# Attention, experts and feed-forward on one core: last four attention blocks as one group, first operands prepared in pieces from step 17 on

## The chip, the cores and the metric

The kernel runs on one core of one Trainium2 chip. The metric is the device time of one execution in microseconds (us); the time given for a kernel is the median of its runs. Five engines of the core matter: PE (TensorE, the matmuls), DVE (VectorE), ACT (ScalarE), POOL (GpSimd) and SP (SyncE, which issues the DMAs). Each engine works through its own list of instructions in order and waits on semaphores for the others.

## The reference

Three stages follow each other. Attention has 2 batches, 8 heads, 576 positions of 64 values, and a bias that a small network computes from the positions; its output is 1152 tokens of 512 values. Then come 8 experts whose weights P are normalised in both directions, and last a feed-forward layer with an ELU.

```python
scores = scale * np.matmul(q, k.transpose(0, 1, 3, 2))
x = (psi_rel / psi_i)[..., None]
bias = np.maximum(x @ w1 + b1, 0.0) @ w2
attn = softmax(scores + bias)
x = np.matmul(attn, v)

for e in range(E):
    h = np.maximum(x @ w1[e], 0.0)
    out += P[:, e:e + 1] * (h @ w2[e])

h = x @ w_in
return np.where(h > 0.0, h, np.exp(np.minimum(h, 0.0)) - 1.0) @ w_out
```

## The kernel before, in words

**Attention in 40 steps.** Two heads form a pair; a pair of one batch is a block, and there are 8 blocks. A block has five query tiles, t = 0 to 3 with 128 rows and t = 4 with 64. One step works on one tile of one block. `groups` lists the blocks that are interleaved: first the four blocks of pairs 0 and 1 (steps 0 to 19, tiles in the order 4, 0, 1, 2, 3), then the two blocks of pair 2 (steps 20 to 29) and the two of pair 3 (steps 30 to 39), tiles 0 to 4.

**What a step does.** `run_step(s)` reads a string letter by letter, and each letter puts instructions on the engines' lists; the order is thus written out by hand. For the scores of step s: `R` and `S` (`emit_ttr`) add the bias on DVE and find the maximum, `E` and `F` (`emit_exp`) take the exponentials of the two heads on ACT, which also sum them. For step s - 1: `T` (`emit_tr`) transposes the exponentials on PE; ACT copies one half of them out of PSUM, and `U` copies the other on DVE. `V` (`emit_trl`) transposes the last 64 columns into one of the two buffers that `T` needs next; ACT empties it at once, behind `F`. For step s - 2 there are five pieces of the product with v, one for each `a`; the fifth also multiplies by the reciprocals of the sums (PE `av<-csb,rc`, line 1332). `X` (`x_evac`) then takes the product out: ACT copies the reciprocals (`xf`), DVE multiplies into the token tile `xt`. `Q` (`emit_qk`) is the score product of step s + 1. `N` (`emit_norm`) makes the reciprocals: GpSimd adds a small number to the sums, and DVE takes the reciprocal at once (line 1265), both for step s - 1; they are used a step later.

**Steps 0 to 13 also compute the bias** for all positions: `H` the hidden layer (`ht`, on DVE or ACT as `pick` decides), `M` its product on PE (`bps`), `O` the copy out of PSUM (`o`, on DVE or ACT) and to DRAM. The string is ORD_S in steps 0 to 2, ORD_A until the bias is complete (steps 3 to 13), and ORD_B from step 14 on. In ORD_A the order on DVE is X, R, S, U, O, H, N, V, H; on PE it is T, a, a, M, a, a, a, V, M, Q.

**First operands of the experts.** Every product runs in three parts of high and low halves. `w_split` prepares one tile of the first expert's weights (`w1h`, `w1l`), `ops_first` one of the token operands (`oh`, `ol`): four sums on GpSimd, four copies to the high half on ACT, four subtractions on DVE for the low half. These are queued in `bg`, and `do_bg` sends one piece for each letter `p`, of which ORD_B has two. The two weight tiles are queued after steps 27 and 28, the two token tiles after steps 35 and 37. What is still queued at the end is sent in one go by `first_fill`, which then starts the planner's list of the experts. `prep` converts q and k of a block (two casts on DVE, two subtractions on DVE or, for blocks 4 to 7, on GpSimd).

```python
ORD_A = "XROTSUapaMEaOHaNpaFLVMHQ"
ORD_B = "RTSNUXaafLEafaappFVQ"
elif x == "N" and 1 <= s <= NS:
    emit_norm(s - 1)
```

Of the kernel before, what the change touches and what calls it, by code (L numbers as in the profile page):

```python
# [34 lines left out]
BD = 1  # L35
PRO = "HHPOH0PpOHpPOHPOkkBHHppPkkppOQmHO"
LQ = [100, 101]
LS = [5, 9, 13, 21]
LV = [0, 1, 2, 3, 19, 20, 28, 32]
ACC = [2.6, 3.1]  # L40
WARM = 8
PS = [[1, 0], [2, 1], [3, 2], [4, 13], [5, 16], [6, 20], [7, 26]]
ORD_S = "RMXTSOHUapaMEOHaaNpMFOHaLVQ"
ORD_A = "XROTSUapaMEaOHaNpaFLVMHQ"
ORD_B = "RTSNUXaafLEafaappFVQ"
TOFF = [0, 128, 256, 384, 512]
TROW = [128, 128, 128, 128, 64]
NN = [256, 320]
# [174 lines left out]
def attention_moe_elu_ffn_kernel(  # L223
# [85 lines left out]
    def w_split():  # L309
        (kind, he, j), t = raw_q.pop(0)  # L310
        hi, lo = wt0[he, j] = w1_new()
        st = stp.tile([128, 4, 2, 128], F32, tag="st", name="st")

        def sums():
            for i in range(4):
                w1_sum(t, st, i, pool)

        def part(i):
            if i:
                dst, src = w1_src(t, st)[i - 1]  # L320
                dve.tensor_tensor(out=lo[:, dst], in0=src, in1=hi.bitcast(F32)[:, dst], op=ALU.subtract)
            if i < 4:
                dst, src = w1_src(t, st)[i]
                act.activation(out=hi[:, dst], in_=src, func=ACTF.Copy)

        bg.extend([sums] + [lambda i=i: part(i) for i in range(5)] + [raw_load])

    def ops_new(n):
        p = xp if n == 0 else pools["ops1"]
# [19 lines left out]
    def ops_first(t):  # L349
        if not ops0:  # L350
            ops0.extend(ops_new(0))
        oh, ol = ops0
        i0, i1 = XPAIR[t]
        xa, xb = ops_view(0, t, xt[i0], xt[i1])
        c = slice(128 * t, 128 * t + 128)
        st = stp.tile([128, 4, 2, 128], F32, tag="st", name="st")

        def part(i):
            if i:
                o, src = ops_src(xa, xb, st)[i - 1]  # L360
                dve.tensor_tensor(out=ol[:, o, :, c], in0=src, in1=oh.bitcast(F32)[:, o, :, c], op=ALU.subtract)
            if i < 4:
                o, src = ops_src(xa, xb, st)[i]
                act.activation(out=oh[:, o, :, c], in_=src, func=ACTF.Copy)

        def sums(i):
            ops_sum(xa, xb, st, i, pool)
            ops_sum(xa, xb, st, i + 1, pool)

        bg.extend([lambda: sums(0), lambda: sums(2)] + [lambda i=i: part(i) for i in range(5)])  # L370

    plan = Plan(0.1)
    eng = {"A": act, "D": dve, "P": pool, "S": sp}
# [750 lines left out]
    emit_it = emit()  # L1124


    groups = [[(hp, b) for hp in (0, 1) for b in range(B)]] + [[(hp, b) for b in range(B)] for hp in range(2, HP)]
    blocks = [hb for grp in groups for hb in grp]
    steps = [(hp, b, t) for i, grp in enumerate(groups) for t in (TO if i == 0 else range(5)) for hp, b in grp]
    gorder = [g for t in TO for g in range(8 * t, min(8 * t + 8, GRP))]  # L1130
# [4 lines left out]
    def attention(fill):  # L1135
# [124 lines left out]
        def emit_norm(s):  # L1260
            sm = etile[s][2]
            r = TROW[steps[s][2]]
            rc = tp.tile([128, 2], F32, tag="rc", name="rc")
            pool.tensor_scalar(rc[0:r], sm[0:r], EPS, None, ALU.add)
            dve.reciprocal(rc[0:r], rc[0:r])
            rcs[s] = rc

        def emit_tr(s):
            r = TROW[steps[s][2]]
# [37 lines left out]
        def av_pieces(s):  # L1307
            hp, b, t = steps[s]
            r = TROW[t]
            box = {}  # L1310

            def piece(j):
                def f():
                    if j == 0:
                        box["p"] = av_p[0] = psC[s % 2 if no[0] == GRP else 0]("av")
                    p = box["p"]
                    vt = vts[hp, b]
                    a = aT[s]
                    for h in range(2):
                        pe.matmul(  # L1320
                            p[64 * h:64 * h + 64, 0:r],
                            vt[:, j - 1 if j else 4, 64 * h:64 * h + 64],
                            a[:, 4 * h + j - 1 if j else 8, 0:r],
                            start=(j == 0),
                            stop=(j == 4),
                            skip_group_check=True,
                        )
                    if j == 4:
                        n, o = XN[b][t], 64 * b if t == 4 else 0
                        rc = rcs.pop(s)  # L1330
                        for h in range(2):
                            pe.matmul(  # L1332
                                p[64 * h:64 * h + 64, 128:128 + r],
                                rc[0:r, h:h + 1].to_broadcast([r, 64]),
                                ident[0:r, 0:r],
                                start=True,
                                stop=True,
                                skip_group_check=True,
                            )
                        ev_q.append((p, r, hp, n, o))  # L1340
                        aT.pop(s)
                return f

            return [piece(j) for j in range(5)]
# [18 lines left out]
        def run_step(s):  # L1363
            d = s - LAG
            cur, tr = s < NS, 0 <= d < NS
            for x in ORD_S if s < 3 else ORD_A if no[0] < GRP else ORD_B:
                if x == "T" and tr:
                    emit_tr(d)
                elif x == "U":
# [6 lines left out]
                elif x in "RS" and cur:  # L1376
                    emit_ttr(s, "RS".index(x))
                elif x in "EF" and cur:
                    emit_exp(s, "EF".index(x))
                elif x == "N" and 1 <= s <= NS:  # L1380
                    emit_norm(s - 1)
                elif x == "X":
                    x_evac()
                elif x == "a":
                    av(1)
                elif x == "M":
                    bias_p()
                elif x == "O":
                    bias_o()
                elif x == "H":  # L1390
                    bias_hh()
                elif x == "p":
                    for _ in range(3 if s < 4 else 1):
                        prep_next()
                    do_bg(1)
                elif x == "L":
                    bias_loads(s)
                elif x == "f":
                    fill_pe(s)
# [139 lines left out]
        for s in range(NS + LAG):  # L1539
# [9 lines left out]
            for i, s0 in PS:  # L1549
                if s == s0:  # L1550
                    prep_q.append(prep(i))
            run_step(s)
            if no[0] < GRP:
                load["a"] += ACC[0]
                load["d"] += ACC[1]
            if s >= NS:
                left.close()
                filler = fill()
                continue
            if s in (20, 22, 24):  # L1560
                raw_load()
            if s == 27:
                w_split()
            if s == 28:
                w_split()
            if s == 15:
                w = csb[:, C_WG:C_WG + 4 * E].rearrange("p (k e) -> p k e", k=4)
                dve.tensor_copy(wg_hl[:, :, 0:E], w)
                dve.tensor_tensor(out=wg_hl[:, :, E:2 * E], in0=w, in1=wg_hl.bitcast(F32)[:, :, 0:E], op=ALU.subtract)
            if s == NS - 5:  # L1570
                ops_first(0)
            if s == NS - 3:
                ops_first(1)
        while av_q:
            x_evac()
            av(3)
# [77 lines left out]
```

## Time and profile before

| | |
|---|---|
| median of 3 runs | 1155.81 us (1154.01 to 1160.21) |
| the profiled execution | 1160.57 us |
| its span | 1158.8 us |
| PE busy | 1127.2 us (97%) |
| DVE busy | 894.3 us (77%) |
| ACT busy | 617.5 us (53%) |
| POOL busy | 48.2 us (4%) |
| mean granted TensorE clock | 0.989 |

The profiled execution takes 1160.57 us, of which its span, from the first to the last instruction, is 1158.8. Attention lies in the first 195 us of it; the rest is the experts and the feed-forward layer. A busy share is an average over the whole span: PE at 97% may still wait in one stage, and an engine that is seldom busy may be the one that others wait for.

### The profile page before, as it was taken

What the parts mean: (1) busy time and instruction counts of PE and PEld (TensorE: products, weight loads), DVE (VectorE), ACT (ScalarE), POOL (GpSimd) and SP (SyncE); (2) the same over time, 40 slices, a digit from 0 to 9 for tenths busy, and PEclk for the clock granted to TensorE, in tenths of its full rate; (3) what the DMA queues carried; (4) which work ended last, traced back from release to release, by engine and by line L of the source; (5) the groups of instructions that cost most, each with busy time, mean ns of one, the idle gap of its engine ahead of it and who ended that gap; (6) DMA issues with size and microseconds to landing.
All of it is one profiled execution on the core that took longest, in us unless ns stands there. A gap on an engine that the chain in (4) does not pass through costs nothing.

```text
span 1158.8 us, 20865 instructions
## 1 busy us (share of the span) xinstructions
PE 1127.2 (97%) x8080; PEld 984.8 (85%) x8080; DVE 894.3 (77%) x1929; ACT 617.5 (53%) x1417; POOL 48.2 (4%) x85
## 2 busy tenths in 40 slices
PE   7899999999999999999999999999999998999998
PEld 3467878988889999999998989998989887989896
DVE  7797887846788888887887878877665568888865
ACT  7897777743234344444443434443434357876653
POOL 0002132000000000000000000000000001000000
PEclk9899998999999999999999999999999999999999
DMA  6564640210122323223323132232111100111002
GB/s 208 194 222 150 201 132 12 75 58 33 55 65 91 110 92 109 91 92 117 102 92 94 64 125 92 91 110 89 58 38 55 51 24 19 55 37 55 19 1 81
DMA packets 36034, 100.14 MB, mean 86 GB/s; under 512 B 3808, under 2 KB 3936, under 8 KB 35936
## 3 DMA queue, kind: packets, MB, share of 16 engines
q1 hardware_dynamic: 35936, 98.82, 26.4%
q8 instruction: 63, 1.03, 0.4%
q14 instruction: 35, 0.29, 0.1%
HBM read 77.16 MB, written 21.64 MB: 85 GB/s over the span
## 4 chain that ended last, share of the span: by engine, by line
PE 88%; ACT 4%; DVE 3%; issue 1%; DVEq 0%; ACTq 0%
PE y L735 41%; PE m L542 38%; PE av L1320 3%; PE sc L1229 2%; PE tr L1281 2%; ACT et L1256 1%; PE bps L1452 1%; ACT ht L1434 1%; PE av L1332 1%; PE trl L1300 0%; ACT o L1484 0%; PE lg L890 0%; ACT aT L1287 0%; DVE ol L442 0%; PE x2t L984 0%
## 5 line engine op out<-in xcount | busy, mean ns | idle before, releaser
L542 PE MATMUL m<-oh,w1h 128*128 128x256 f32 (+1 forms) x1120 | 331.1, 296 | 1.2 <-ACT u L555 1.2
L542 PE MATMUL m<-ol,w1h 128*128 128x256 f32 (+1 forms) x1120 | 330.3, 295 | 0.1
L542 PE MATMUL m<-oh,w1l 128*128 128x256 f32 (+1 forms) x1120 | 329.9, 295 | 0.0
L735 PE MATMUL y<-w2h,hh 128*128 128x512 f32 x720 | 282.2, 392 | 2.3 <-ACT hh L649 1.1
L735 PE MATMUL y<-w2l,hh 128*128 128x512 f32 x720 | 281.6, 391 | 0.8 <-DVE w2l L442 0.8
L735 PE MATMUL y<-w2h,hl 128*128 128x512 f32 x720 | 281.5, 391 | 0.0
L542 PEld LDWEIGHTS m<-oh,w1h 128*128 128x128 f32 x1120 | 211.2, 189 | 9.0 <-ACT u L555 1.7
L542 PEld LDWEIGHTS m<-ol,w1h 128*128 128x128 f32 x1120 | 211.0, 188 | 8.1 <-DVE ol L442 0.6
L542 PEld LDWEIGHTS m<-oh,w1l 128*128 128x128 f32 x1120 | 211.3, 189 | 0.1
L735 PEld LDWEIGHTS y<-w2h,hh 128*128 128x128 f32 x720 | 135.1, 188 | 27.5 <-ACT hh L649 2.0
L735 PEld LDWEIGHTS y<-w2h,hl 128*128 128x128 f32 x720 | 135.2, 188 | 26.7 <-DVE hl L652 0.2
L735 PEld LDWEIGHTS y<-w2l,hh 128*128 128x128 f32 x720 | 135.2, 188 | 24.5 <-DVE w2l L442 1.1
L605 ACT ACTIVATE hh<-c 128x512 fp32r<-128x512 f32 (+3 forms) x128 | 72.0, 563 | 144.9 <-DVE c L574 144.7
L766 DVE SCALAR_TENSOR_TENSOR acc<-y,P,acc 128x512 f32<-128x512 f32 x126 | 94.6, 751 | 65.8 <-PE y L735 64.4
L555 ACT ACTIVATE u<-m 128x256 f32<-128x256 f32 (+1 forms) x160 | 64.9, 405 | 86.2 <-PE m L542 84.4
L555 ACT ACTIVATE p<-m 128x256 f32<-128x256 f32 (+1 forms) x160 | 65.6, 410 | 71.1 <-PE m L542 66.2
L608 DVE SCALAR_TENSOR_TENSOR hl<-c,hh 128x512 fp32r<-128x512 f32 (+3 forms) x128 | 77.7, 607 | 20.1 <-ACT hh L605 17.4
L435 ACT ACTIVATE w2h<-raw 128x512 fp32r<-128x512 f32 x80 | 48.5, 627 | 51.1 <-PE y L735 50.4
L1241 DVE CUSTOM_DVE_ANT_0 et<-sc,bt 128x576 f32<-128x576 f32 (+1 forms) x80 | 57.2, 752 | 17.1 <-PE sc L1229 15.3
L435 ACT ACTIVATE w1h<-st 128x512 fp32r<-128x512 f32 x76 | 46.5, 623 | 33.9 <-DVE st L307 32.2
L1256 ACT ACTIVATE et<-et,nmx 128x576 f32<-128x576 f32 (+1 forms) x80 | 61.8, 776 | 0.7 <-DVE nmx L1241 0.7
L574 DVE TENSOR_TENSOR c<-m,u 128x256 f32<-128x256 f32 (+1 forms) x80 | 36.6, 457 | 32.2 <-PE m L542 29.6
(140 smaller groups left out, 1516.4 us busy)
## 6 DMA issues: line engine op xcount, KB each, us to landing
raw<-w1p SPq DMA_DIRECT2D x32, 512.0 KB, 3.9
raw<-w2p SPq DMA_DIRECT2D x32, 512.0 KB, 3.3
scr<-o SPq DMA_DIRECT2D x36, 295.5 KB, 2.5
bt<-scr SPq DMA_DIRECT2D x16, 576.0 KB, 4.3
cw<-w1d SPq DMA_DIRECT2D x16, 512.0 KB, 4.1
wsc<-ca SPq DMA_DIRECT2D x32, 256.0 KB, 4.0
cw<-w2d SPq DMA_DIRECT2D x16, 512.0 KB, 4.1
raw<-wsc SPq DMA_DIRECT2D x16, 512.0 KB, 3.6
```

The lines of the kernel that those rows point to most:

```text
L435: act.activation(out=dst(bh.get()), in_=src(), func=ACTF.Copy)
L542: lambda e, w=w, o=o, j=j, k=k: pe.matmul(x["ap"](bank), w.get()[:, ai, j, :], o.get()[:, bi, j, :], start=(k == 0 and i in (1, 2, 5)), st ...
L555: lambda e: act.activation(out=b.get()[:, 0:N], in_=x["ap"](bank), func=ACTF.Copy),
L574: lambda e: eng[e].tensor_tensor(out=blk(b.get()[:, half * N:half * N + N], rev), in0=ap(p), in1=ap(q), op=ALU.add),
L605: op([("A", cA(w))], lambda e: act.activation(out=hh(), in_=ap(), func=ACTF.Relu), r=sk, w=wh, after=gate_)
L608: lambda e: dve.scalar_tensor_tensor(out=bl.get()[:, d], in0=ap(), scalar=0.0, in1=hhf(), op0=ALU.max, op1=ALU.subtract),
L735: lambda e, a=a, w=w, f=f, i=i, y=y, c=c: pe.matmul(y.get(), a.get()[:, c], w.get(), start=(f == 0 and i == 0), stop=(f == 3 and i == 2)),
L766: lambda e: dve.scalar_tensor_tensor(out=a.get(), in0=y.get(), scalar=P[0][:, n, e_:e_ + 1], in1=a.get(), op0=ALU.mult, op1=ALU.add),
L1229: pe.matmul(sc[h][0:r, x, 0:HALF], q[d, qc], k[d, kc], start=i == 0, stop=i == 2, tile_position=(64 * h, 0))
L1241: dve.tensor_tensor_reduce(out=e.rearrange("p (x j) -> p x j", x=2), in0=sc[0:r, :, 0:HALF], in1=biast[hp, t][0:r, h].rearrange("p (x j) - ...
L1256: act.activation(out=e, in_=e, func=ACTF.Exp, scale=-1.0, bias=nmx[0:r, h:h + 1], accum_out=sm[0:r, h:h + 1])
L1320: pe.matmul(p[64 * h:64 * h + 64, 0:r], vt[:, j - 1 if j else 4, 64 * h:64 * h + 64], a[:, 4 * h + j - 1 if j else 8, 0:r], start=(j == 0) ...
```

## The change

The four blocks of pairs 2 and 3 become one group of steps 20 to 39: tiles 0 of four blocks, then tiles 1, and so on, so that the four tiles of 64 rows come last. `BG` queues the weight tiles before steps 17 and 22 and the token tiles before steps 27 and 32. A piece is sent by the new letter `g`, one in a step; ORD_B has one `g`, between `E` and `F`, and its two `p` only prepare q and k. The four subtractions of each tile go to GpSimd, and the sums move into the pieces. Loads of q, k, v and of the first weights are issued earlier. `N` still adds on GpSimd for step s - 1, but the reciprocal on DVE, now `emit_recip`, is that of step s - 2, in all three strings. The last step has a string of its own, ORD_E, and the planner's list is started before it, so that its letters `f` send products of the first expert. The products with v of the last two steps use the same PSUM buffer.

```diff
@@ -35,14 +35,16 @@
 BD = 1
 PRO = "HHPOH0PpOHpPOHPOkkBHHppPkkppOQmHO"
 LQ = [100, 101]
-LS = [5, 9, 13, 21]
-LV = [0, 1, 2, 3, 19, 20, 28, 32]
+LS = [5, 8, 11, 14]
+LV = [0, 1, 2, 3, 19, 20, 21, 22]
+BG = [17, 22, 27, 32]
 ACC = [2.6, 3.1]
 WARM = 8
-PS = [[1, 0], [2, 1], [3, 2], [4, 13], [5, 16], [6, 20], [7, 26]]
+PS = [[1, 0], [2, 1], [3, 2], [4, 13], [5, 16], [6, 17], [7, 18]]
 ORD_S = "RMXTSOHUapaMEOHaaNpMFOHaLVQ"
 ORD_A = "XROTSUapaMEaOHaNpaFLVMHQ"
-ORD_B = "RTSNUXaafLEafaappFVQ"
+ORD_B = "RTSNUXaaLEaaappgFVQ"
+ORD_E = "XffTUNaafaaaV"
 TOFF = [0, 128, 256, 384, 512]
 TROW = [128, 128, 128, 128, 64]
 NN = [256, 320]
@@ -316,14 +318,18 @@
                 w1_sum(t, st, i, pool)
 
         def part(i):
-            if i:
+            if i == 0:
+                sums()
+            else:
                 dst, src = w1_src(t, st)[i - 1]
-                dve.tensor_tensor(out=lo[:, dst], in0=src, in1=hi.bitcast(F32)[:, dst], op=ALU.subtract)
+                pool.tensor_tensor(out=lo[:, dst], in0=src, in1=hi.bitcast(F32)[:, dst], op=ALU.subtract)
             if i < 4:
                 dst, src = w1_src(t, st)[i]
                 act.activation(out=hi[:, dst], in_=src, func=ACTF.Copy)
-
-        bg.extend([sums] + [lambda i=i: part(i) for i in range(5)] + [raw_load])
+            else:
+                raw_load()
+
+        bg.extend([lambda i=i: part(i) for i in range(5)])
 
     def ops_new(n):
         p = xp if n == 0 else pools["ops1"]
@@ -356,18 +362,17 @@
         st = stp.tile([128, 4, 2, 128], F32, tag="st", name="st")
 
         def part(i):
+            if i < 2:
+                ops_sum(xa, xb, st, 2 * i, pool)
+                ops_sum(xa, xb, st, 2 * i + 1, pool)
             if i:
                 o, src = ops_src(xa, xb, st)[i - 1]
-                dve.tensor_tensor(out=ol[:, o, :, c], in0=src, in1=oh.bitcast(F32)[:, o, :, c], op=ALU.subtract)
+                pool.tensor_tensor(out=ol[:, o, :, c], in0=src, in1=oh.bitcast(F32)[:, o, :, c], op=ALU.subtract)
             if i < 4:
                 o, src = ops_src(xa, xb, st)[i]
                 act.activation(out=oh[:, o, :, c], in_=src, func=ACTF.Copy)
 
-        def sums(i):
-            ops_sum(xa, xb, st, i, pool)
-            ops_sum(xa, xb, st, i + 1, pool)
-
-        bg.extend([lambda: sums(0), lambda: sums(2)] + [lambda i=i: part(i) for i in range(5)])
+        bg.extend([lambda i=i: part(i) for i in range(5)])
 
     plan = Plan(0.1)
     eng = {"A": act, "D": dve, "P": pool, "S": sp}
@@ -1124,7 +1129,7 @@
     emit_it = emit()
 
 
-    groups = [[(hp, b) for hp in (0, 1) for b in range(B)]] + [[(hp, b) for b in range(B)] for hp in range(2, HP)]
+    groups = [[(hp, b) for hp in hps for b in range(B)] for hps in ((0, 1), (2, 3))]
     blocks = [hb for grp in groups for hb in grp]
     steps = [(hp, b, t) for i, grp in enumerate(groups) for t in (TO if i == 0 else range(5)) for hp, b in grp]
     gorder = [g for t in TO for g in range(8 * t, min(8 * t + 8, GRP))]
@@ -1260,10 +1265,12 @@
         def emit_norm(s):
             sm = etile[s][2]
             r = TROW[steps[s][2]]
-            rc = tp.tile([128, 2], F32, tag="rc", name="rc")
+            rc = rcs[s] = tp.tile([128, 2], F32, tag="rc", name="rc")
             pool.tensor_scalar(rc[0:r], sm[0:r], EPS, None, ALU.add)
-            dve.reciprocal(rc[0:r], rc[0:r])
-            rcs[s] = rc
+
+        def emit_recip(s):
+            rc = rcs[s][0:TROW[steps[s][2]]]
+            dve.reciprocal(rc, rc)
 
         def emit_tr(s):
             r = TROW[steps[s][2]]
@@ -1312,7 +1319,7 @@
             def piece(j):
                 def f():
                     if j == 0:
-                        box["p"] = av_p[0] = psC[s % 2 if no[0] == GRP else 0]("av")
+                        box["p"] = av_p[0] = psC[1 if s >= NS - 2 else s % 2 if no[0] == GRP else 0]("av")
                     p = box["p"]
                     vt = vts[hp, b]
                     a = aT[s]
@@ -1363,7 +1370,7 @@
         def run_step(s):
             d = s - LAG
             cur, tr = s < NS, 0 <= d < NS
-            for x in ORD_S if s < 3 else ORD_A if no[0] < GRP else ORD_B:
+            for x in ORD_S if s < 3 else ORD_A if no[0] < GRP else ORD_B if cur else ORD_E:
                 if x == "T" and tr:
                     emit_tr(d)
                 elif x == "U":
@@ -1377,8 +1384,11 @@
                     emit_ttr(s, "RS".index(x))
                 elif x in "EF" and cur:
                     emit_exp(s, "EF".index(x))
-                elif x == "N" and 1 <= s <= NS:
-                    emit_norm(s - 1)
+                elif x == "N":
+                    if 1 <= s <= NS:
+                        emit_norm(s - 1)
+                    if 2 <= s:
+                        emit_recip(s - 2)
                 elif x == "X":
                     x_evac()
                 elif x == "a":
@@ -1392,6 +1402,7 @@
                 elif x == "p":
                     for _ in range(3 if s < 4 else 1):
                         prep_next()
+                elif x == "g":
                     do_bg(1)
                 elif x == "L":
                     bias_loads(s)
@@ -1549,28 +1560,25 @@
             for i, s0 in PS:
                 if s == s0:
                     prep_q.append(prep(i))
+            if s == NS:
+                left.close()
+                filler = fill()
             run_step(s)
             if no[0] < GRP:
                 load["a"] += ACC[0]
                 load["d"] += ACC[1]
             if s >= NS:
-                left.close()
-                filler = fill()
                 continue
-            if s in (20, 22, 24):
+            if s in (15, 16, 17):
                 raw_load()
-            if s == 27:
-                w_split()
-            if s == 28:
-                w_split()
+            if s + 1 in BG:
+                i = BG.index(s + 1)
+                w_split() if i < 2 else ops_first(i - 2)
             if s == 15:
                 w = csb[:, C_WG:C_WG + 4 * E].rearrange("p (k e) -> p k e", k=4)
                 dve.tensor_copy(wg_hl[:, :, 0:E], w)
                 dve.tensor_tensor(out=wg_hl[:, :, E:2 * E], in0=w, in1=wg_hl.bitcast(F32)[:, :, 0:E], op=ALU.subtract)
-            if s == NS - 5:
-                ops_first(0)
-            if s == NS - 3:
-                ops_first(1)
+        emit_recip(NS - 1)
         while av_q:
             x_evac()
             av(3)
```

How instructions move, in two places. The first is DVE in step 10, from the copy of the transposed exponentials (`aT<-tr`) to that of the last 64 columns (`aT<-av`). The number behind a name tells tiles apart. Before:

```order
L1371 COPY aT_1217<-tr_1219 128x8x64
L1486 TENSOR_SCALAR o_1252<-bps_1244,csb_87 128x176
L1486 TENSOR_SCALAR o_1252<-bps_1244,csb_87 128x415
L1436 TENSOR_SCALAR ht_152<-U_134,csb_87 128x448
L1436 TENSOR_SCALAR ht_153<-U_134,csb_87 128x448
L1265 RECIPROCAL rc_1262<-rc_1262 128x2
L1303 COPY aT_1217<-av_1239 128x64
```

Now:

```order
L1378 COPY aT_1216<-tr_1218 128x8x64
L1497 TENSOR_SCALAR o_1251<-bps_1243,csb_87 128x176
L1497 TENSOR_SCALAR o_1251<-bps_1243,csb_87 128x415
L1447 TENSOR_SCALAR ht_152<-U_134,csb_87 128x448
L1447 TENSOR_SCALAR ht_153<-U_134,csb_87 128x448
L1273 RECIPROCAL rc_1169<-rc_1169 128x2
L1310 COPY aT_1216<-av_1238 128x64
```

Nothing moved but the tile of the reciprocal: it was rc_1262, it is rc_1169. PE's list in the same step uses rc_1169 before and now; this is its part now:

```order
L1463 MATMUL bps_1243<-ht_153,csb_87 32x416
L1463 MATMUL bps_1243<-ht_154,csb_87 32x416 x3
L1327 MATMUL av_1238<-aT_1124,vt_298 64x128 x6
L1339 MATMUL av_1238<-csb_87,rc_1169 64x128 x2
L1307 MATMUL trl_1271<-csb_87,et_1098 128x64
L1307 MATMUL av_1238<-csb_87,et_1098 128x64
L1463 MATMUL bps_1276<-ht_151,csb_87 32x432 x3
L1463 MATMUL bps_1276<-ht_152,csb_87 32x432
```

PE thus reads a reciprocal that DVE made in the step before; now it reads the one that DVE makes in this step, behind the copies `o` and the hidden layers `ht`.

The second place is ACT where the first weight tile is copied. Before, in steps 28 to 30, whose first exponentials are those of the 64-row tiles:

```order
L1256 ACTIVATE et,sm<-et,nmx 64x576
L324 ACTIVATE w1h<-raw 128x512
L1256 ACTIVATE et,sm<-et,nmx 64x576
L1305 ACTIVATE aT<-trl 128x64
L1287 ACTIVATE aT<-tr 128x4x64
L1350 ACTIVATE xf<-av 128x128
L1256 ACTIVATE et,sm<-et,nmx 64x576
L324 ACTIVATE w1h<-raw 128x256
L324 ACTIVATE w1h<-st 128x512
L1256 ACTIVATE et,sm<-et,nmx 64x576
```

Now, in steps 17 and 18:

```order
L1261 ACTIVATE et,sm<-et,nmx 128x576
L328 ACTIVATE w1h<-raw 128x512
L1261 ACTIVATE et,sm<-et,nmx 128x576
L1312 ACTIVATE aT<-trl 128x64
L1294 ACTIVATE aT<-tr 128x8x64
L1357 ACTIVATE xf<-av 128x128
L1261 ACTIVATE et,sm<-et,nmx 128x576
L328 ACTIVATE w1h<-raw 128x256
L1261 ACTIVATE et,sm<-et,nmx 128x576
```

The copies still stand between the two exponentials, one in a step at most, and eleven steps earlier.

## Rows read from the trace of the kernel before

**Rows 1.** DVE's instructions in order of time, step 10: start us, us, engine, what.

```profile
80.33 0.75 DVE L1241 CUSTOM_DVE_ANT_0 et<-sc,bt 128x576 f32<-128x576 f32 x1
...
83.87 0.16 DVE L1265 RECIPROCAL rc<-rc 128x2 f32<-128x2 f32 x1
```

**Rows 2.** PE's instructions in order of time, where step 10 reads its reciprocals.

```profile
82.69 0.39 PE L1332 MATMUL av<-csb,rc 128*64 128x128 f32 x4
```

**Rows 3.** PE's instructions in order of time, end of step 12.

```profile
93.35 0.39 PE L1332 MATMUL av<-csb,rc 128*64 128x128 f32 x4
...
93.88 1.04 PE L1452 MATMUL bps<-ht,csb 128*32 128x496 f32 x8
94.85 0.40 PE L1229 MATMUL sc<-kh,qh 64*128 64x288 f32 x2
```

**Rows 4.** DVE's instructions in order of time: reciprocals of steps 3 and 13, scores of step 13.

```profile
48.85 0.15 DVE L1265 RECIPROCAL rc<-rc 64x2 f32<-64x2 f32 x1
...
95.94 0.76 DVE L1241 CUSTOM_DVE_ANT_0 et<-sc,bt 128x576 f32<-128x576 f32 x1 [0.52 <-PE sc L1229]
...
98.27 0.16 DVE L1265 RECIPROCAL rc<-rc 128x2 f32<-128x2 f32 x1
```

**Rows 5.** DVE then PE in order of time, where PE waits for DVE's `xt`.

```profile
102.13 0.28 DVE L1351 TENSOR_TENSOR xt<-av,xf 128x128 f32<-128x128 f32 x1
...
102.56 1.85 PE L1320 MATMUL av<-aT,vt 128*64 128x128 f32 x20 [1.97 <-DVE xt L1351]
```

**Rows 6.** PE's longest waits in the stretch 105 to 200 us: total, times, longest.

```profile
PE tr L1281 <- ACT aT L1305: 4.4, 7, 0.9
```

**Rows 7.** ACT's instructions in order of time, steps 33 to 35.

```profile
164.68 0.22 ACT L1305 ACTIVATE aT<-trl 128x64 f32<-128x64 f32 x1
...
167.11 1.15 ACT L324 ACTIVATE w1h<-st 128x512 fp32r<-128x512 f32 x2
168.91 0.22 ACT L1305 ACTIVATE aT<-trl 128x64 f32<-128x64 f32 x1
169.93 0.60 ACT L1287 ACTIVATE aT<-tr 128x512 f32<-128x512 f32 x1 [0.80 <-PE tr L1281]
...
172.10 0.22 ACT L1305 ACTIVATE aT<-trl 128x64 f32<-128x64 f32 x1
```

**Rows 8.** DVE in order of time, step 17: reciprocal in ORD_B.

```profile
114.35 0.16 DVE L1265 RECIPROCAL rc<-rc 128x2 f32<-128x2 f32 x1
```

**Rows 9.** PE in order of time: step 17, then the products of a 64-row tile.

```profile
113.56 1.31 PE L1320 MATMUL av<-aT,vt 128*64 128x128 f32 x20
114.70 0.39 PE L1332 MATMUL av<-csb,rc 128*64 128x128 f32 x4
...
189.81 0.80 PE L1320 MATMUL av<-aT,vt 128*64 128x64 f32 x20
190.54 0.33 PE L1332 MATMUL av<-csb,rc 64*64 64x64 f32 x4
```

**Rows 10.** DVE, then GpSimd, in order of time: low halves of the last token tile.

```profile
191.71 1.28 DVE L361 TENSOR_TENSOR ol<-xt,oh 128x512 fp32r<-128x512 f32 x1
...
193.25 0.68 DVE L361 TENSOR_TENSOR ol<-st,oh 128x512 fp32r<-128x512 f32 x1
...
191.70 0.74 POOL L340 TENSOR_TENSOR st<-xt,st 128x256 f32<-128x256 f32 x1
```

**Rows 11.** PE in order of time: two waits, with what ended them.

```profile
45.97 0.46 PE L1281 MATMUL tr<-csb,et 64*128 64x64 f32 x4 [1.03 <-ACT aT L1305]
...
191.81 0.84 PE L1320 MATMUL av<-aT,vt 128*64 128x64 f32 x12 [0.73 <-ACT oh L364]
```

**Rows 12.** Busy time by stretch: us, PE, PEld, DVE, ACT, POOL, then the granted clock.

```profile
46.00:48.00 2.00, 2.00 (x32) 1.19 (x32) 1.94 (x7) 1.31 (x5) 0.00 (x0) 1.00 0.98 214
...
195.00:197.00 2.00, 2.00 (x13) 1.85 (x12) 1.32 (x4) 0.74 (x2) 0.00 (x0) 0.50 0.04 8
104.00:106.00 2.00, 2.00 (x18) 1.67 (x17) 0.23 (x1) 0.23 (x1) 0.00 (x0) 0.50 0.47 179
```

## The prediction

> **What bounds the kernel now.** I read the page first: PE is busy for 97% of the span, and only attention, the first 195 us, has stretches where it waits. Then I read DVE, PE and ACT in order of time through attention, step by step, and after that the waits and the granted clock.
>
> In steps 3 to 13 (48 to 99 us) a step takes about 5 us. The reader is to see two rows of step 10: DVE takes the reciprocal at 83.87 [rows 1], and PE multiplies by reciprocals at 82.69 [rows 2], 1.2 us earlier. That does no harm today, since PE reads the tile that DVE made a step before.
>
> From step 14 on a step takes 3.19 us, and a ring through ACT sets it. From one ACT copy of the 64-column transposes to the next, 168.91 to 172.10, lie 3.19 us, and ACT's only idle time in it is 0.80 us for PE's transposes, which wait for that very copy [rows 7]. With two weight copies (1.04 us of spacing) in the ring the distance is 4.23, from 164.68 to 168.91: all of it is added [rows 7]. Seven such waits of PE sum to 4.4 us [rows 6].
>
> [...]
>
> **The change part by part.**
>
> *The reciprocal a step later.* It is the smallest edit and the largest term. PE's multiplication by the reciprocals in step s now needs what DVE writes in the same step, behind scores, copies, `o` and `ht`. In step 10 DVE reaches it at 83.87; it lasts 0.16, and PE starts 0.15 after DVE ends where it waits for DVE (102.13 + 0.28, then 102.56) [rows 5]. So PE starts at 84.18 instead of 82.69 and waits 1.5 us. Queued behind it on PE are the 64-column transposes, a bias product and the scores of the next step; DVE's next step waits for those scores, and its next reciprocal stands behind them. That closes a ring, whose length is the new step:
>
> - DVE's reciprocal to PE: 0.16 + 0.15 = 0.31 [rows 5];
> - PE, from this multiplication to the bias product: 93.35 to 93.88, 0.53 [rows 3];
> - the bias product: 0.97 in step 12, 93.88 to 94.85 [rows 3]; for steps 3 to 12 it is 0.65 to 0.97, ten together 7.85;
> - from the start of the next scores to DVE's first instruction on them, where DVE waits for nothing else: 94.85 to 95.94, 1.09 [rows 3, 4];
> - from there to the reciprocal on DVE, all of it work: 3.54 in step 10, 80.33 to 83.87 [rows 1], 2.33 in step 13, 95.94 to 98.27 [rows 4]; for steps 4 to 13 ten of them, together 32.95.
>
> From the reciprocal of step 3 to that of step 13 this makes 10 x (0.31 + 0.53 + 1.09) + 7.85 + 32.95 = 60.1 us. Today it is 98.27 - 48.85 = 49.4 [rows 4]. **The term is +10.7.** In step 13 PE wants the reciprocal no earlier than DVE has it, so the delay stays and doesn't grow. From below: with a handover of 0.21 instead of 0.31 it is +9.7. ACT could be a second ring, since `xf` waits for the same multiplication, but it comes out just shorter than PE's, so nothing is added for it.
>
> *Copies of the first operands on ACT.* All 16 now lie in the ring of ACT, in steps 17 to 35, one to a step. A copy of 512 columns costs 0.52 there (half of 1.04 [rows 7]), one of 256 columns about 0.3, an estimate from it. Four tiles of three large copies and one small make 4 x 1.86 = 7.4 us, against 4.4 of PE's waits today [rows 6]: **+3.0**. Spreading them saves nothing while ACT is the ring. The lower end is -4.4, if every copy fitted into the 0.80 us that ACT idles.
>
> *Subtractions to GpSimd.* DVE isn't in this ring, so what it loses is worth nothing; what covers GpSimd is that no result is wanted before the products at the end. GpSimd has about 7.5 us of work for a tile in five steps of 3.2 to 3.7 us, and in steps 17, 19 and 21 the subtractions for q and k, 2.9 us each. It falls behind by up to 3 us in step 17; the additions for the sums queue behind that, but their reciprocal is taken in the step after next. The cost is 0, and that delay is what the later reciprocal pays for in ORD_B. One row is a warning: a subtraction of 512 columns on DVE took 1.28 us while GpSimd ran a sum, 0.68 alone [rows 10]. DVE's subtractions are gone, but six casts stay, four of them beside GpSimd, and no row shows a cast beside it. The nearest price is that row's 0.6 for each, 2.4 us together on DVE, which isn't the bound in those steps; I take 0 and keep 2.4 for the range. [...]
>
> *Four 64-row tiles at the end.* In a full step of ORD_B DVE has the reciprocal at 114.35 [rows 8], and with 0.31 PE could start at 114.66; it gets there at 114.70 [rows 9], so the later reciprocal just fits. For a 64-row tile PE needs 0.73 (189.81 to 190.54) instead of 1.14 (113.56 to 114.70) for the products before it [rows 9], and its transposes are half. It then waits about 0.6 us in two steps and half of that in one: **+1.4**, 0 from below.
>
> *The last step.* Token operands are ready, so products of the first expert follow directly. The wait of 0.73 goes [rows 11]. If PE stays at its upper clock, the 6.7 us from 191.9 to 198.6 at half clock [rows 12] shrink by half: -3.4. Together **-4.1**; 0 if another wait there takes its place. The candidate is the PSUM buffer that the last two steps now share.
>
> The moved DMAs (q, k, v, weights on SP's queue) find their buffers free long before, and no wait of PE in this stretch is for a DMA: 0.
>
> **Sum**: 10.7 + 3.0 + 0 + 1.4 - 4.1 = +11.0. It is worked out against the profiled execution of 1160.57 us (span 1158.8), which lies 4.8 above the median of 1155.81. On the median it gives 1155.8 + 11.0 = **1166.8 us**.
>
> **The rivals.**
>
> *The clock falls in steps 3 to 12.* PE's new waits there are 0.9 to 1.8 us, one in each step. After 1.03 us of waiting at 45.97 the clock stayed at 1.00; after 1.97 at 102.56 it was 0.50 [rows 5, 11, 12]. The new waits lie between. In a step at half clock the bias product, the scores and the multiplication in the ring take about 2.4 us longer, after which PE has no gap left and the clock should return. If five of the ten steps fall, that is +12: 1179. The point is whether a single wait of about 1.3 us is enough.
>
> *The copies fit, and the late reciprocal costs nothing: faster.* If ACT's idle 0.80 [rows 7] took one copy of 0.52 each, the 4.4 us of waits would go altogether, with the end's 4.1: -8.5, 1147.3. It decides at one copy in a step, which is less than 0.80. Against it: that idle time is ACT waiting for PE's transposes, which wait for ACT's copy, and 1.04 of copies made the step 1.04 longer. It also needs PE to reach the reciprocals after DVE in steps 3 to 12, against rows 1 and 2.
>
> *The wait is there, but half is swallowed.* If DVE's part of the ring shrinks or the fall of the clock at 102.56 goes away, and the end gains its 4.1, about +3 is left: 1159, no change.
>
> *The change doesn't do what it says:* the lists show the reciprocal, the pieces and the order of steps as described, so this gets no chance.
>
> **How the numbers follow.** Forecast 0.62, fallen clock 0.19, half swallowed 0.13, faster 0.06. About 0.5% (5.8 us) is what a measurement of this kernel can tell from no change. The forecast's own bounds are +7 (handover 0.21, waits of the 64-row tiles 0, and some copies hidden) to +17 (clock falls again at the end, 2.4 of casts): 1162.8 to 1172.8. To hold 8 in 10 the range runs down to the half-swallowed case and up to nearly all of the fallen clock: 1159 to 1178. Faster by over 0.5%: 0.06. Within 0.5%: 0.13 and a little of the forecast's lower end, 0.15. Slower: 0.79.
>
> **What would show it.** In the changed profile PE's multiplication by reciprocals should be listed as waiting for DVE's reciprocal, ten times, over 0.8 us each and some 14 us in all, and steps 4 to 12 should last 5.6 to 6.5 us; DVE should idle before `aT<-av`. The stretch to step 13 should end about 10.7 us later. In steps 17 to 35 distances between ACT's copies should be 3.7 with a large piece and 3.2 without. After 190 us there should be no half clock. The prediction is wrong if PE doesn't wait at that line, or if steps 17 to 35 stay at 3.19.

## The result, and the profile after

The changed kernel takes **1171.57 us** (median of 6 runs, 1171.19 to 1175.15), the kernel before beside it 1155.74 (6 runs, 1154.01 to 1160.21): ratio 1.0136, 95% interval 1.0115 to 1.0157, **slower by 15.8 us**. Measured again later beside the experiments it took 1170.11, ratio 1.0113 (1.0094 to 1.0132), or 13.1 us. The forecast was 1166.8 in a range of 1159 to 1178, with slower at 0.79. Direction and range held; the sum, +11.0, was too small.

First the page of the changed kernel: its span, its engines' busy times, and the clock by slices.

```profile
span 1169.7 us, 20843 instructions
...
PE 1125.8 (96%) x8080; PEld 981.9 (84%) x8080; DVE 888.3 (76%) x1913; ACT 618.6 (53%) x1417; POOL 65.6 (6%) x101
...
PEclk9999999999999999999999999999999999999999
```

PE is busy for as long as before, within 1.4 us: the time went into waits, and GpSimd's 17 more microseconds aren't where it shows. PE's waits say where: the first row is of 0 to 110 us, the three below it of 110 to 215 (total, times, longest).

```profile
PE av L1339 <- DVE rc L1273: 10.8, 10, 1.6
...
PE tr L1288 <- ACT aT L1312: 6.4, 16, 0.8
PE av L1327 <- DVE xt L1358: 2.6, 2, 2.0
PE av L1339 <- DVE rc L1273: 0.8, 2, 0.4
```

The first row is new, ten waits in ten steps; `tr` behind `aT` stood at 4.4 in seven waits [rows 6] and is now 6.4 in sixteen. The step where the reader saw DVE come 1.2 us behind PE [rows 1, 2] reads like this now, DVE first, then PE:

```profile
85.30 0.22 DVE L1310 COPY aT<-av 128x64 f32<-128x64 f32 x1 [0.77 <-PE av L1307]
...
87.07 0.76 DVE L1246 CUSTOM_DVE_ANT_0 et<-sc,bt 128x576 f32<-128x576 f32 x1
...
90.62 0.16 DVE L1273 RECIPROCAL rc<-rc 128x2 f32<-128x2 f32 x1
...
90.84 0.44 PE L1339 MATMUL av<-csb,rc 128*64 128x128 f32 x4 [1.07 <-DVE rc L1273]
91.21 0.27 PE L1307 MATMUL trl<-csb,et 64*128 64x64 f32 x1
91.21 0.27 PE L1307 MATMUL av<-csb,et 64*128 64x64 f32 x1
91.41 0.93 PE L1463 MATMUL bps<-ht,csb 128*32 128x432 f32 x8
92.28 0.40 PE L1234 MATMUL sc<-kh,qh 64*128 64x288 f32 x2
```

That is the ring on two engines: PE waits 1.07 for the reciprocal, the next scores stand behind that, and DVE idles 0.77 before the copy that needs PE's small transposes. PE starts 0.22 after DVE's reciprocal starts.

One of the ten steps is longer than this ring by itself makes it. The longest of the ten waits, 1.56 us in step 5, is followed by half clock: PE's rows come first, then DVE's first instruction on the scores that PE makes there, and by itself PE's busy time from 61 to 63 us, with the granted clock as the third number from the right.

```profile
59.71 0.33 PE L1339 MATMUL av<-csb,rc 64*64 64x64 f32 x4 [1.56 <-DVE rc L1273]
...
60.18 1.16 PE L1463 MATMUL bps<-ht,csb 128*32 128x320 f32 x8
61.27 0.61 PE L1234 MATMUL sc<-kh,qh 64*128 64x288 f32 x2
...
62.87 1.05 PE L1288 MATMUL tr<-csb,et 64*128 64x64 f32 x16
...
63.11 0.76 DVE L1246 CUSTOM_DVE_ANT_0 et<-sc,bt 128x576 f32<-128x576 f32 x1 [1.36 <-PE sc L1234]
```

```profile
61.00:63.00 2.00, 2.00 (x20) 0.50 0.35 120
```

From the reciprocal of step 5 to that of step 6 (59.51 to 66.69) it takes 7.2 us, where the parts of the ring at the upper clock make 5.9 (0.21 + 0.46 + 0.68 in the second profile, 1.10 as in the step before, 3.44 in the kernel before): 1.3 of the +11.4 that the table below shows for these steps is clock. The second profile of the changed kernel, whose longest wait there is 1.6 too, and that of the kernel before with nothing but the late reciprocal (experiment 2) show as much of it: the granted clock from 40 to 95 us is 0.97 in each of the three, and 1.00 in both profiles of before. The other nine waits, 0.57 to 1.28, are followed by 1.00, and behind the longest the clock is back there from 65 us on.

ACT, which sets the later steps [rows 7], three steps of them:

```profile
122.54 0.60 ACT L1294 ACTIVATE aT<-tr 128x512 f32<-128x512 f32 x1 [0.80 <-PE tr L1288]
...
123.95 0.63 ACT L328 ACTIVATE w1h<-raw 128x512 fp32r<-128x512 f32 x1
...
126.25 0.60 ACT L1294 ACTIVATE aT<-tr 128x512 f32<-128x512 f32 x1 [0.81 <-PE tr L1288]
...
127.66 0.41 ACT L328 ACTIVATE w1h<-raw 128x256 fp32r<-128x256 f32 x1
...
129.75 0.60 ACT L1294 ACTIVATE aT<-tr 128x512 f32<-128x512 f32 x1 [0.81 <-PE tr L1288]
```

The step with a large copy lasts 3.71, that with a small one 3.50, against 3.19 without; the idle 0.80 stays whole in each. And the end, PE in order of time:

```profile
197.94 0.33 PE L1339 MATMUL av<-csb,rc 64*64 64x64 f32 x4 [0.38 <-DVE rc L1273]
...
201.34 0.39 PE L547 MATMUL m<-oh,w1h 128*128 128x256 f32 x1
...
206.59 0.57 PE L1327 MATMUL av<-aT,vt 128*64 128x64 f32 x12 [0.69 <-DVE xt L1358]
...
209.35 0.29 PE L895 MATMUL lg<-oh,wg_hl 128*16 128x256 f32 x1 [0.64 <-DVE xt L1358]
```

The wait of 0.73 [rows 11] has given way to 0.69 for the shared PSUM buffer and 0.64 for the last `xt`.

**The whole difference by stage.** PE's first scores of steps 3, 14 and 17 and ACT's first `hh` (the first thing that the experts make) are marks that every kernel has. Here they are for the changed kernel, and for a second profile of the kernel before:

```profile
42.71 0.40 PE L1234 MATMUL sc<-kh,qh 64*64 64x288 f32 x2
...
109.47 0.38 PE L1234 MATMUL sc<-kh,qh 64*128 64x288 f32 x2
...
120.78 0.38 PE L1234 MATMUL sc<-kh,qh 64*128 64x288 f32 x2
...
211.37 0.62 ACT L610 ACTIVATE hh<-c 128x512 fp32r<-128x512 f32 x1
```

```profile
42.03 0.40 PE L1229 MATMUL sc<-kh,qh 64*64 64x288 f32 x2
...
97.39 0.38 PE L1229 MATMUL sc<-kh,qh 64*128 64x288 f32 x2
...
110.23 0.38 PE L1229 MATMUL sc<-kh,qh 64*128 64x288 f32 x2
...
196.88 0.62 ACT L605 ACTIVATE hh<-c 128x512 fp32r<-128x512 f32 x1
```

From the first `hh` to the end of the span every profile of this study needs 957.6 to 958.7 us, so all but 1 us of the difference arises before it. The same marks in all thirteen profiles (us; each ratio is to runs of before taken beside that kernel):

| kernel | to step 3 | 3 to 14 | 14 to 17 | 17 to `hh` | median | ratio to before (95%) |
|---|---|---|---|---|---|---|
| before | 43.64 | 55.38 | 12.89 | 89.19 | 1155.81 | |
| before, second profile | 42.03 | 55.36 | 12.84 | 86.65 | 1157.07 | 0.9991 (0.9977 to 1.0006) |
| changed | 42.71 | 66.76 | 11.31 | 90.59 | 1171.57 | 1.0136 (1.0115 to 1.0157) |
| changed, second profile | 40.98 | 66.76 | 11.32 | 90.59 | 1170.11 | 1.0113 (1.0094 to 1.0132) |
| 1: changed, early reciprocal | 40.87 | 55.39 | 11.27 | 90.55 | 1159.18 | 1.0015 (1.0001 to 1.0029) |
| 2: before, late reciprocal | 42.82 | 66.75 | 11.33 | 86.38 | 1166.40 | 1.0072 (1.0054 to 1.0091) |
| 3: as 1, copies on DVE | 41.88 | 55.40 | 12.77 | 85.46 | 1155.20 | 0.9980 (0.9966 to 0.9994) |
| 4: as 1, copies on GpSimd | 41.29 | 55.40 | 12.85 | 83.66 | 1152.53 | 0.9962 (0.9945 to 0.9979) |
| 5: as 1, early to the end | 43.59 | 55.39 | 12.79 | 90.23 | 1159.14 | 1.0021 (1.0003 to 1.0038) |
| 6: as 1, DVE subtracts | 41.86 | 55.40 | 12.77 | 90.54 | 1159.84 | 1.0020 (1.0005 to 1.0036) |
| 7: before, copies on GpSimd | 42.00 | 55.36 | 12.86 | 85.87 | 1156.21 | 0.9987 (0.9971 to 1.0003) |
| 8: as 4, other buffer | 46.02 | 55.38 | 9.45 | 83.91 | 1151.64 | 0.9943 (0.9921 to 0.9965) |
| 9: as 8, tail early | 41.19 | 55.38 | 9.43 | 83.43 | 1149.59 | 0.9929 (0.9910 to 0.9949) |

The column "3 to 14" repeats to 0.04 us within either kind of kernel. "To step 3" scatters by 5 us between executions: PE's granted clock from 24 to 40 us was 0.57 and 0.73 in the two profiles of before, 0.79 and 0.89 in those of the changed kernel, and 0.50 to 1.00 elsewhere.

### The profile page after: what moved, and what is told of

Read it like the earlier page. It is cut to its first block, busy times and chain, and to the rows that moved or that the text cites. A ratio compares the mean times of both kernels' runs of the same rounds, so it can differ in the third digit from the quotient of the medians.

```text
span 1169.7 us, 20843 instructions
## 1 busy us (share of the span) xinstructions
PE 1125.8 (96%) x8080; PEld 981.9 (84%) x8080; DVE 888.3 (76%) x1913; ACT 618.6 (53%) x1417; POOL 65.6 (6%) x101
## 4 chain that ended last, share of the span: by engine, by line
PE 84%; DVE 6%; ACT 5%; issue 1%; DMA 1%; DVEq 0%; ACTq 0%; SPq 0%
PE y L740 40%; PE m L547 37%; ACT et L1261 2%; PE sc L1234 2%; PE tr L1288 1%; PE av L1327 1%; PE bps L1463 1%; DVE et L1246 1%; PE av L1339 1%; ACT aT L1294 1%; DVE ht L1447 1%; DVE o L1497 1%; DMA raw<-w1p 1%; PE lg L895 0%; DVE aT L1378 0%
```

## The experiments

**Theory A**: the late reciprocal makes a ring in steps 3 to 12 (about +11), the copies lengthen ACT's ring (+3), and the rest of the surprise lies in the profiled execution of before, at 1160.57 above its median. **Rival 1**: the clock falls in steps 3 to 12. **Rival 2**: GpSimd's subtractions or the earlier loads disturb DVE and PE.

**The kernel before once more**, no edit.

> The kernel before, unchanged, for its clocks and a second profile. Theory A (the late reciprocal costs about 11 us, the copies 3, and the profiled execution of before, at 1160.57, held stretches of half clock that the median execution does not have): about 1155.7, with mean clocks near 0.995 in most executions, and a profile near the median should show fewer half-clock stretches in attention than the first one. If instead the half clock at 192 to 198 us belongs to the kernel, a second profile shows it there again.

The wait at the end is there again, the fall behind it isn't. PE in order of time, and then its busy time from 194 to 199 us, with the granted clock as the third number from the right:

```profile
100.93 2.40 PE L1320 MATMUL av<-aT,vt 128*64 128x128 f32 x20 [1.97 <-DVE xt L1351]
...
190.12 0.57 PE L1320 MATMUL av<-aT,vt 128*64 128x64 f32 x12 [0.73 <-ACT oh L364]
190.62 0.38 PE L542 MATMUL m<-oh,w1h 128*128 128x256 f32 x1
```

```profile
194.00:199.00 5.00, 5.00 (x46) 1.00 0.00 0
```

The same 0.73 us was followed by 0.50 in the first profile [rows 11, 12] and by 1.00 in this one; 17 to `hh` is 2.5 us shorter. So that half clock does not come in every execution of this kernel. The one at step 14 did come again (2.40 us for products that take 1.31 at the upper clock).

**1. The reciprocal at once in the first group.**

```diff
+            early = s < 3 or no[0] < GRP
...
-                    if 2 <= s:
+                    if early and 1 <= s:
+                        emit_recip(s - 1)
+                        rec.add(s - 1)
+                    elif 2 <= s and s - 2 not in rec:
                         emit_recip(s - 2)
```

> The changed kernel, but the reciprocals of the steps of the first group are taken at once again, as before. Theory A: the ring from DVE's reciprocal through PE's scores and back is gone in steps 3 to 12, so 10.5 to 11.4 us below the changed kernel, about 1160.6; PE's waits for the reciprocal sum to about 1 us instead of 11.6, and the reciprocal of step 13 is 49.4 us after that of step 3. Rival 1 (it is the clock): the time falls only by what fallen clock the changed kernel has in steps 3 to 12, one stretch of about 1.3 us, so about 1170. Rival 2 (GpSimd's subtractions or the earlier loads disturb these steps): about 1170 too, with the waits still there.

1159.18, 10.9 below the second measurement of the changed kernel. Its waits, from 0 to 215 us:

```profile
PE tr L1288 <- ACT aT L1312: 7.5, 17, 1.0
...
PE av L1339 <- DVE rc L1273: 0.8, 2, 0.4
```

3 to 14 is 55.39, as in the kernel before, with subtractions, loads and groups as changed. Rival 2 falls. Of rival 1 the 1.3 us of step 5 stand: with the wait that half clock is gone too (1.00 from 40 to 95 us). The other 10 are the ring's.

**2. The late reciprocal alone, in the kernel before.**

```diff
             pool.tensor_scalar(rc[0:r], sm[0:r], EPS, None, ALU.add)
-            dve.reciprocal(rc[0:r], rc[0:r])
-            rcs[s] = rc
+        def emit_recip(s):
+            rc = rcs[s][0:TROW[steps[s][2]]]
+            dve.reciprocal(rc, rc)
```

(with the calls as in the change)

> The kernel before, with the reciprocal taken one step later and nothing else. Theory A: 10.7 to 11.4 us above the kernel before, 1166.4 to 1167.1, up to 2 more if its groups with 64-row tiles inside make PE wait there too; PE waits for the reciprocal in ten steps, about 11 us in all. Rivals 1 and 2: no more than 2 us above, about 1157.

8.4 us slower (6.3 to 10.5), under what was expected. The stages tell why: 3 to 14 grows by 11.4, but 14 to 17 shrinks by 1.5. In all three profiles with late reciprocals the clock stays up at step 14 (1.00 from 95 to 120 us), behind a wait of 1.96 and 1.97 us in the two of the changed kernel; in seven of the eight with early ones that have this wait, it falls to half behind it (0.89 from 95 to 110 us in each), and in kernel 1, behind 1.91, it is 1.00.

**3. Copies on DVE** (to kernel 1).

```diff
-                act.activation(out=hi[:, dst], in_=src, func=ACTF.Copy)
+                dve.tensor_copy(hi[:, dst], src)
```

(and the same for `oh`)

> The kernel with the early reciprocals in the first group, and the copies of the first operands (16 of them, in steps 17 to 35) on DVE instead of ACT. Theory A: ACT is the ring of these steps and every copy is added to it, so the steps last 3.19 us again and 7.4 us go: about 1153.2, below the kernel before. Against it, if DVE is near its limit there or GpSimd's subtractions slow its copies: steps of 3.4 us and about 1157; if the copies were not in the ring at all: no change, about 1160.6.

1155.2: 4.0 below kernel 1, and 5.1 in the stretch from 17 to `hh`, where 7.4 was hoped for. Most steps are 3.19 again, but one lasts 4.76 and one 4.05. DVE, GpSimd and PE in the long one, and a copy beside an idle GpSimd:

```profile
117.80 1.35 DVE L328 CAST w1h<-raw 128x256 fp32r<-128x256 f32 x1
...
138.48 0.42 DVE L328 CAST w1h<-st 128x512 fp32r<-128x512 f32 x1
...
117.64 1.35 POOL L325 TENSOR_TENSOR w1l<-raw,w1h 128x512 fp32r<-128x512 f32 x1
...
119.33 1.31 PE L1327 MATMUL av<-aT,vt 128*64 128x128 f32 x20 [1.19 <-DVE aT L1310]
```

The smaller copy took three times as long as the larger and ended at 119.15, 0.16 after GpSimd's subtraction; behind it on DVE stood `aT`, which PE wanted. The step of 4.05 has another cause, a bias load that came 0.97 us late.

**4. Copies on GpSimd** (to kernel 1, and the same for `oh`).

```diff
-                act.activation(out=hi[:, dst], in_=src, func=ACTF.Copy)
+                pool.tensor_copy(hi[:, dst], src)
```

> The kernel with early reciprocals in the first group, and the 16 copies of the first operands on GpSimd, so that neither the ring on ACT nor DVE pays for them. Theory A: steps 17 to 35 last 3.19 us but where DVE's casts for q and k run beside GpSimd; from step 17 to the first hh copy 83.2 to 84.5 us (with copies on ACT 90.55, on DVE 85.46), the time 1 to 2 below the kernel with copies on DVE, about 1153.5. Against it: GpSimd has about 11 us of work for a tile in five steps of 3.2, falls behind in steps 17 to 22, and the additions for the sums come too late even for the later reciprocal: 2 to 6 us of PE's waits, about 1157.

17 to `hh` is 83.66, inside what Theory A gave, and 1152.53 is 0.4% below the kernel before (0.2% to 0.6%). Against kernel 3 the gain shows in that stretch, 1.8 us; the intervals of the two ratios overlap. GpSimd does not fall too far behind: PE waits for a reciprocal only at the 64-row tiles. From step 17 on only steps 19 and 21 (3.72, 3.67) are over 3.25, those in which DVE's casts for q and k meet GpSimd's work and take 0.63 to 0.86 in place of 0.45.

**5. The reciprocal at once in the second group too** (to kernel 1).

```diff
-            early = s < 3 or no[0] < GRP
+            early = True
...
-        emit_recip(NS - 1)
```

> As the kernel with early reciprocals in the first group, and early ones in the second group too. If the later reciprocal pays for GpSimd's delay there, as the prediction has it: DVE waits for GpSimd's additions in steps 17, 19 and 21 by up to 3 us each, and the time is 2 to 5 above that kernel, about 1163. If not: the two waits of 0.38 at the 64-row tiles go and the time is 0.8 below it or the same, about 1158.5.

The same time (1.0021 against 1.0015), which the second case allowed; the first fails. DVE waits for GpSimd once:

```profile
119.02 0.17 DVE L1273 RECIPROCAL rc<-rc 128x2 f32<-128x2 f32 x1 [1.54 <-POOL rc L1269]
```

It lengthens a step from 3.50 to 4.10, and at the 64-row tiles 0.9 comes back. The delay that the later reciprocal was to pay for is worth 0.6 us.

**6. Subtractions on DVE** (to kernel 1, and the same for `ol`).

```diff
-                pool.tensor_tensor(out=lo[:, dst], in0=src, in1=hi.bitcast(F32)[:, dst], op=ALU.subtract)
+                dve.tensor_tensor(out=lo[:, dst], in0=src, in1=hi.bitcast(F32)[:, dst], op=ALU.subtract)
```

> As the kernel with early reciprocals in the first group, with the 16 residual subtractions on DVE as before the change. Theory A: DVE isn't in the ring of steps 17 to 35, so the same within 0.5 us: 90.55 us from step 17 to the first hh copy. Rival 2 (GpSimd's subtractions disturb DVE and so PE): at least 1 us less.

90.54 against 90.55, and the medians are 0.7 apart, well inside the spread of their runs. On which engine they run is worth nothing.

**The changed kernel once more**, no edit.

> The changed kernel, unchanged, beside the others and with a second profile. By the starts of the scores of a step in the profiles so far: +11.3 us from step 3 to step 14 against the kernel before, +3.9 from step 17 to the first hh copy on ACT, and from there to the end the same to 1 us. Theory A: these two stretches come out within 0.2 us again (74.4 and 90.6 us), and the time lies 11 to 15 above the kernel before, the clock's stretches making the rest. If the clock had made the +11.3, that stretch should scatter by more than 1 us between two profiles.

66.76 and 90.59, to 0.01 as in the first profile. (The 74.4 was counted from the scores of step 2, and the clock before step 3 moved that one by 0.4.) +13.1 is inside the expectation.

**7. Before, with copies on GpSimd alone**: the diff of kernel 4, in the kernel before.

> The kernel before with one edit: the 16 copies of the first operands on GpSimd instead of ACT; groups, order, reciprocals and the last step stay. From step 17 to the first hh copy it took 86.65 us in the second profile of before and 83.66 in the changed kernel with GpSimd's copies. If ACT's copies are all that this stretch can gain: 82.2 to 83.7 us and about 1153.5, as good as that kernel, and the one group, the pieces over the steps and the products in the last step are worth nothing. If those parts are worth something by themselves: 84.5 or more, about 1155.5, or a new wait of PE at the end for copies that GpSimd makes too late.

85.87 and 1156.21: no change that the interval shows. Its last step, PE in order of time:

```profile
186.46 0.91 PE L1320 MATMUL av<-aT,vt 128*64 128x64 f32 x12 [1.21 <-DVE xt L1351]
187.70 0.58 PE L542 MATMUL m<-oh,w1h 128*128 128x256 f32 x1 [0.33 <-POOL oh L364]
```

For GpSimd's copies PE waits 0.33 us, and soon after 0.31 for a low half that DVE makes from one. The longer wait before that, 1.21, is for DVE's `xt`, behind a reciprocal that waits 2.02 us for GpSimd's addition, as it did in the second profile of before. The granted clock from 188 to 194 us is 0.59; in the nine profiles with the changed last step it is 1.00 from 178 to 210 us. So copies off ACT alone are not shown to pay, and kernel 4 needs 2.2 us less from 17 to `hh`. Which of its other parts makes that (the one group, the pieces spread out, the subtractions on GpSimd, the later reciprocal, the last step), and how much of it is clock, isn't separated.

**8. The other PSUM buffer first** (to kernel 4).

```diff
-psC[1 if s >= NS - 2 else s % 2 if no[0] == GRP else 0]("av")
+psC[1 if s >= NS - 2 else (s + 1) % 2 if no[0] == GRP else 0]("av")
```

> The kernel with early reciprocals in the first group and copies on GpSimd, and the two PSUM buffers of the av products of the second group taken in the other order, so that step 14 doesn't take the buffer that the step before it used. The wait of 1.9 us there goes. If the half clock behind it comes of that wait: 14 to 17 lasts 9.4 to 9.7 us instead of 12.85, the granted clock stays at 1.00, and the time is 3.3 lower, about 1149.2. If the clock falls there without the wait: 1.9 lower, about 1150.6.

PE's busy time and granted clock in step 14, in kernel 4, and then here, where the step begins 4.7 us later:

```profile
100.00:103.00 3.00, 2.85 (x28) 0.57 0.93 255
```

```profile
104.00:107.00 3.00, 3.00 (x54) 1.00 0.79 208
```

14 to 17 falls from 12.85 to 9.45: the wait of 1.9 is gone, and the half clock with it. The median, 1151.64, is higher than hoped, with runs from 1149.04 to 1155.72; the profiled one had 46.02 us to step 3. The gain thus shows in the stage and not in the medians: the intervals of kernels 4 and 8 overlap.

**9. The tail's reciprocals at once** (to kernel 8; no reciprocal is taken twice).

```diff
-            early = s < 3 or no[0] < GRP
+            early = s < 3 or no[0] < GRP or s > NS - 4
```

> As the kernel with the buffers in the other order, with the reciprocals of the 64-row tiles at the end taken at once. The two waits of 0.38 go: 0.8 below that kernel, about 1148.4, if PE's end isn't held by DVE's last xt; 0 if it is.

17 to `hh` is 0.48 shorter and the time 1149.59, **0.7% faster than before** (0.5% to 0.9%) and 20.5 us below the second measurement of the changed kernel. That it beats kernel 8 isn't shown by the medians; their intervals overlap.

## Why the prediction was right, and where it was not

- **The ring of the reciprocal** was right in mechanism and place: +10.7 predicted, +11.4 measured from step 3 to 14, and from the reciprocal of step 3 to that of step 13 (47.91 to 108.72) 60.8 against 60.1. Two sizes were off and nearly cancelled, which is luck: the handover is 0.22, not 0.31, which takes 0.9 off, and the half clock of step 5, which this term had at nothing, adds 1.3. The waits are 10.8 in ten, not 14, and one of them (0.57) is under 0.8.
- **The clock** did what the rival feared, but in one step of ten where it had priced five, and for 1.3 us where it had priced 2.4. At step 14, where the kernel before fell to half clock in both its profiles, the changed kernel did not, which gave back 1.5. The sum had neither, and they cancel.
- **ACT's copies**: right. 0.52 and 0.31 in the ring, +7.4 for sixteen. The 4.4 set against it is a sum of PE's waits, and not of added length as the 7.4 is: by waits the sixteen stand at 6.4.
- **GpSimd's subtractions**: 0, as predicted (experiment 6). The casts beside GpSimd do suffer: in the changed kernel two of those for q and k took 0.76 and 0.93 in place of 0.45, near the 0.6 kept for the range; in experiment 3 a copy took 1.35 where a larger one alone took 0.42. Where the copies lie on ACT they are off the path.
- **The 64-row tiles**: two waits of 0.38, 0.8 in place of 1.4.
- **The last step** is the term that failed: -4.1. Its -3.4 took half clock of one execution for a property of the kernel; its -0.7 was taken by the wait named as its candidate, the shared buffer. From step 17 to `hh` the terms give +0.3 with it, and +4.4 without; measured is +3.9 against the second profile of before, +1.4 against the first.

Against the profiled execution the sum was exact, +11.0 for +10.9, and that is luck as well. The stages of the two profiles give -0.9 to step 3, then +11.4, -1.6, +1.4, and +0.6 behind `hh`; the sum had +10.7 for the second, +0.3 for the fourth and nothing for the others. That execution was 4.8 us above its median, and 2.5 of it by the second profile was the half clock at the end that the sum counted as a gain; carried over to the median, the sum came out 4.8 too low by the first measurement and 2.1 by the second. By stages against the second profile: +11.4 - 1.5 + 3.9 = +13.8, and 13.1 and 15.8 were measured.

## What to carry to other kernels

An operation that is moved "a step later" costs nothing only if its reader also has a step to spare: compare its place on its engine with its reader's place on the other, and where the reader comes first, sum the ring. Work that one engine carries in a ring isn't made cheaper by spreading it; it must go to an engine outside the ring, and what reads its results must come late enough to cover that engine's delay: here the sixteen copies, one to a step, cost 0.52 or 0.31 us each on ACT, and on GpSimd the stretch from step 17 to `hh` fell from 90.55 to 83.66. Before a stall of one profiled execution is counted as a gain, see whether a second profile has it: here +11.0 met the one, by luck, and was 2.8 short of the stages measured against the other.

## What the runs showed of the hardware

- **DVE's casts took longer beside GpSimd's tensor instructions.** In kernel 3 a cast of 512 columns took 0.42 us beside an idle GpSimd; the seven copies of the first operands that met one of GpSimd's tensor instructions took 0.76 to 1.35, the longest with 256 columns. The two whose times are shown beside GpSimd's, 1.35 and 0.76 us, ended 0.16 and 0.14 after its subtraction. GpSimd's subtractions of 512 columns took 1.27 to 1.35, and 1.28 in the mean where ACT made the copies (kernel 1). What makes the casts longer is not shown.
- **The same wait is not always followed by half clock**: 0.73 us at the end with (0.50) and without (1.00), 1.91 to 1.98 us at step 14 in seven of eight profiles with early reciprocals (0.89 from 95 to 110 us) and in none of three with late ones (1.00). Those three have 0.97 from 40 to 95 us instead, in the changed kernel behind 1.56 us at step 5. Why is open; that it goes when the wait goes is shown: 1.00 in step 5 of kernel 1 and in step 14 of kernel 8.
